# Decode attention with a parallel GLU on one Trainium2 core: head 0's K loaded in halves, two heads ahead of DVE's loop, eight rows of w_o on DVE, other pieces of w_down and w_o

## The chip, the cores and the metric

The kernel runs on one core of a Trainium2 chip. The core has five engines that run at the same time and tell each other of their progress by semaphores: PE (TensorE, matrix products), DVE (VectorE), ACT (ScalarE), POOL (GpSimd) and SP (SyncE, which here only issues transfers). 16 DMA engines bring data from the main memory into the core's own memory (128 partitions). The metric is the device time of one execution in microseconds (us), lower is better.

## The reference

One token is decoded. A cached attention and a gated feed-forward part both start from the same normalised input, and their outputs are added to it. All numbers are 32-bit floats.

```python
# x: (1,1,576); k_cache, v_cache: (1,32,16384,128); wq: (576,4096); wo: (4096,576)
# w_gate, w_up: (576,4608); w_down: (4608,576)
xn = layernorm(x)
q = (xn @ wq) as (1, 32 heads, 1, 128)
scores = einsum("bhqd,bhkd->bhqk", q, k_cache) * 128 ** -0.5
o = einsum("bhqk,bhkd->bhqd", softmax(scores), v_cache)
attention = o.reshape(1, 1, 4096) @ wo
h = gelu(xn @ w_gate) * (xn @ w_up)
return x + attention + h @ w_down
```

K and V of one head are 8.39 MB each, so 32 heads make 537 MB of the 588 MB that the kernel reads.

## The kernel before

The program writes out one list of instructions per engine (class `Plan`): `op` adds an instruction with the events it has to wait for, `dma` a transfer, `call` a hand-written loop. Every engine works through its list strictly in order. All large transfers are issued by SP, in the order of its list, to one queue.

Three large regions of memory, A, B and C, are used again and again. The input weights (wq, w_gate, w_up) lie in them first. Then K of even heads goes to region B (tile `kb`, which is `kt[0]`), K of odd heads to region A (`ka`, `kt[1]`), and V of every head to region C (`vt`). At the end the regions take w_down and w_o: `wd0` in B, `wd1` and `wo0` in A, `wo1` in B behind `wd0`, whose memory it uses again.

Start. PE computes q, the gate and the up part while the weights arrive (L210 to 253). The first K may be loaded when the gate part no longer needs region B (`done[0]`), the second K and the first V when the up part is through (`done[1]`). ACT writes the first head's q, spread over all partitions, to `qb0` (L277).

Heads. For each of 32 heads DVE (L302 to 315) waits for the head's K (semaphore `k0` or `k1`) and its q (`qb`), multiplies K by q in place (L308), sums over the 128 numbers of a key (L310, tile `sc`), and takes a maximum (L313, L315). `take` waits for a semaphore and takes its count back. With L312 (`s_kf`) DVE tells SP that the K tile is free. ACT makes the exponentials (L327), PE multiplies them with V (L292, "the PV product", tile `po`), ACT copies `po` out (L329) and PE folds it to one column per head (L297). With its first folding matmul PE tells SP (`s_vf`) that V's tile is free. So SP's order is V0, K2, V1, K3 and so on: K of head h + 2 waits for DVE's sums of head h, V of head h for the PV product of the head before.

Tail. The last transfers on SP's list are, in this order: V30, `wd0` (24 rows of w_down, when DVE has read K30), V31, `wd1` (12 rows, when DVE has read K31), three pieces of w_o of 6, 5 and 5 rows in region A, and eight pieces of 6, 4 and six times 1 row in region B, which wait until DVE has used `wd0`. A row here is 576 numbers on each of 128 partitions. DVE adds up the rows of w_down, each times a column of `hT`, in `wacc` (`down`, L355): first the rows of `wd0`, then, behind the normalisation of the attention output (L377 to L383, tile `oT`), the rows of `wd1`. PE takes the rows of w_o, two matmuls each (`out_rows`, L387): the first 26 into four groups of `acc`, the last six into `fin`. In PE's list the sum over the partitions of `wacc` goes to `fin` behind row 22 (`SUMS`), the sum of `acc` (copied to `part` by DVE, L403) behind row 27. DVE and ACT copy `fin` to `osb` (L406, L407), and SP stores it.

Of the kernel before, what the change touches and what calls it, by code (L numbers as in the profile page):

```python
# [9 lines left out]
ALU = mybir.AluOpType  # L10
AX = mybir.AxisListType
PE = mybir.EngineType.PE

P = 128
H, SK, DH = 32, 16384, 128
D, DF = 576, 4608
N = SK // P
# [8 lines left out]
WT = HD // P  # L26
CUT = ((0, 11), (11, 22), (22, 32))
S0 = 32512
SLOT = 4 * N * DH
WD1 = 24  # L30
WO1 = 16
WO_CUTS = (6, 5, 5, 6, 4, 1, 1, 1, 1, 1, 1)
LAST = 6
SUMS = 22


class Plan:
# [13 lines left out]
    def op(self, e, fn, *deps, sig=None, by=1):  # L51
        if e in ("dve", "act", "pool"):
            deps += (self.last.get(e),)
        sig = sig or self.own[e]
        self.count[sig.name] = self.count.get(sig.name, 0) + by
        self.q[e].append((deps, fn, sig, by))
        if sig is self.own[e]:
            self.last[e] = sig, self.count[sig.name]
        return sig, self.count[sig.name]

    def dma(self, e, out, in_, *deps, sem=None):
        sem = sem or self.sem(f"d{len(self.count)}")
        return self.op(e, lambda g: g.dma_start(out, in_), *deps, sig=sem, by=16)
# [27 lines left out]
def take(g, sem, n=1):  # L91
    g.wait_ge(sem, n).then_inc(sem, -n)  # L92
# [8 lines left out]
def plan(nc, pl, x, k_cache, v_cache, wq, wo, wg, wu, wd, out):  # L101
    op, dma = pl.op, pl.dma
    kv = k_cache.rearrange("b h (p n) d -> (b h) p (n d)", p=P)
# [23 lines left out]
    ident, ones = small("ident", [P, P]), small("ones", [P, P])  # L127
# [7 lines left out]
    qb = [small(f"qb{i}", [P, DH]) for i in range(2)]  # L135
    sc = [small(f"sc{i}", [P, N]) for i in range(2)]
    pm, nm, nb, pe = small("pm", [P, 1]), small("nm", [1, 1]), small("nb", [P, 1]), small("pe", [P, N])
    ls, o4 = small("ls", [P, H + 1]), small("o4", [P, 512])
    oall, oT = small("oall", [P, H + 1]), small("oT", [P, WT])
# [5 lines left out]
    wacc, part = small("wacc", [P, 2, HALF], over), small("part", [P, 2, HALF], over + 4 * D)  # L145
# [7 lines left out]
    kt = [big("kb", N * DH, B), big("ka", N * DH, A)]  # L153
    vt = big("vt", N * DH, C)
    wd0, wd1 = big("wd0", WD1 * D, B), big("wd1", (FT - WD1) * D, A)
    wo0, wo1 = big("wo0", WO1 * D, A + 4 * (FT - WD1) * D), big("wo1", (WT - WO1) * D, B)

# [5 lines left out]
    po, pqb, pt, pb, pc, acc, fin = banks(("po", 1), ("pqb", 1), ("pt", 1), ("pb", 1), ("pc", 1), ("acc", 2), ("fin", 1))  # L163
    px = pu[:, 0, :]

    s_hs, s_pm, s_nm, s_p, s_o4, s_v = (pl.sem(n) for n in ("hs", "pm", "nm", "p", "o4", "v"))
    s_pq, s_pt, s_pb, s_pv, s_pc = (pl.sem(n) for n in ("pq", "pt", "pb", "pv", "pc"))
    s_qb, s_ol, s_kf, s_vf, s_d, s_a = (pl.sem(n) for n in ("qb", "ol", "kf", "vf", "d", "a"))
    s_k = [pl.sem(f"k{i}") for i in range(2)]


# [21 lines left out]
    for i in range(2):  # L193
        k = op("dve", lambda g, i=i: g.bn_stats(st[:, i, :], xrow[:, i * HALF : (i + 1) * HALF]), d_x)
    k = op("dve", lambda g: g.bn_aggr(mv, st), k)
    k = op("act", lambda g: g.activation(std, mv[:, 1:2], AF.Sqrt, bias=eps[:1], scale=1.0), k, c_eps)
    k = op("dve", lambda g: g.reciprocal(rstd, std), k)
# [3 lines left out]
    for j in range(DJ):  # L201
        k = op("pe", lambda g, j=j: g.matmul(px[:, j : j + 1], xm[:, j, :], ones[:1, :1], start=True, stop=True), k_xn, c_ones)
    k = op("pe", lambda g: g.matmul(px[:, DJ : DJ + 1], xd.rearrange("o d s -> o (d s)"), ones[:1, :1], start=True, stop=True), k_xd)
    k = op("dve", lambda g: g.tensor_copy(xp, px[:, : DJ + 1]), k)
    k_xnb = op("dve", lambda g: g.tensor_copy(xnb, xp[:, :DJ].unsqueeze(2).to_broadcast([P, DJ, 32])), k)
    k = op("dve", lambda g: g.tensor_scalar(xt, par, xp[:, DJ:], None, op0=ALU.mult), k, c_par)
# [20 lines left out]
    rows = [(wqm[:, j * HD : (j + 1) * HD], d_q[0]) for j in range(DJ)]  # L227
# [18 lines left out]
    done = []  # L246
    for i, (dst, pieces, t) in enumerate(((pg, gp, (gt, d_g[2])), (pu, up, (ut, d_ut)))):
        view = []
        for b, (lo, hi) in enumerate(CUT):
            k = wide(dst, b, (FT * lo, FT * hi), pieces, t, FQ)  # L250
# [9 lines left out]
    k = op("dve", lambda g: g.tensor_mul(t1, g_, g_), k_f)  # L260
    k = op("dve", lambda g: g.tensor_scalar(t1, t1, 0.044715, 1.0, op0=ALU.mult, op1=ALU.add), k)
    k = op("dve", lambda g: g.tensor_mul(t1, t1, g_), k)
    k = op("act", lambda g: g.activation(th, t1, AF.Tanh, scale=0.7978845608028654), k)
    k = op("dve", lambda g: g.scalar_tensor_tensor(t2, th, 1.0, g_, op0=ALU.add, op1=ALU.mult), k)
    k_h = op("dve", lambda g: g.scalar_tensor_tensor(hT, t2, 0.5, u_, op0=ALU.mult, op1=ALU.mult), k)
# [9 lines left out]
    k = op("act", lambda g: pick(g, 0), c_h)  # L275
# [4 lines left out]
    def on_pe(g):  # L280
        with g.Fori(0, H):
# [17 lines left out]
                    m.then_inc(s_vf, 1)  # L299
            m.then_inc(s_pc, 1)  # L300

    def on_dve(g):  # L302
        with g.Fori(0, H // 2):  # L303
            for i in range(2):
                kd = kt[i].rearrange("p (n d) -> p n d", d=DH)
                take(g, s_k[i], 16)
                take(g, s_qb)
                g.tensor_mul(kd, kd, qb[i].unsqueeze(1).to_broadcast([P, N, DH])).then_inc(s_d, 1)  # L308
                take(g, s_d)
                g.tensor_reduce(sc[i], kd, axis=AX.X, op=ALU.add).then_inc(s_d, 1)  # L310
                take(g, s_d)
                g.sem_inc(s_kf, 1)  # L312
                g.tensor_reduce(pm, sc[i], axis=AX.X, op=ALU.max).then_inc(s_pm, 1)  # L313
                take(g, s_pt)
                g.tensor_reduce(nm, pt[:1, 0, :P], axis=AX.X, op=ALU.max, negate=True).then_inc(s_nm, 1)  # L315

    def on_act(g):
        with g.Fori(0, H, 2) as h2:
# [18 lines left out]
    def load_k(h, *deps):  # L337
        dma("sp", kt[h % 2], kv[h], *deps, sem=s_k[h % 2])
# [1 line left out]
    def load_v(h):  # L340
        dma("sp", vt, vv[h], (s_vf, h) if h else done[1], sem=s_v)

    load_k(0, done[0])
    load_k(1, done[1])
    for h in range(H - 2):
        load_v(h)
# [5 lines left out]
    k_o = s_ol, H  # L352


    def down(lo, hi, w, dep, k):  # L355
        for t in range(lo, hi):
            r, c = w[:, (t - lo) * D : (t - lo + 1) * D], hT[:, t : t + 1]
            o = wacc.rearrange("p a f -> p (a f)")
            if t == 0:
                k = op("dve", lambda g, r=r, c=c: g.tensor_scalar(o, r, c, None, op0=ALU.mult), dep, k_h)  # L360
            else:
                k = op("dve", lambda g, r=r, c=c: g.scalar_tensor_tensor(o, r, c, o, op0=ALU.mult, op1=ALU.add), dep, k)  # L362
        return k

    k_w0 = down(0, WD1, wd0, d_wd0, None)
    d_wo, lo = [], 0
    for n in WO_CUTS:
        w, base, dep = (wo0, 0, (s_kf, H)) if lo < WO1 else (wo1, WO1, k_w0)
        c = w[:, (lo - base) * D : (lo - base + n) * D]
        d = dma("sp", c, wov[:, lo * D : (lo + n) * D], dep)  # L370
# [5 lines left out]
    k = op("pe", lambda g: g.matmul(pqb[:, 0, :H], ones, ls[:, :H], start=True, stop=True))  # L376
    k = op("dve", lambda g: g.reciprocal(rl, pqb[:, 0, :H]), k)  # L377
    k = op("dve", lambda g: g.tensor_mul(oexp, oall[:, :H].unsqueeze(2).to_broadcast([P, H, 4]),
                                         rl.unsqueeze(2).to_broadcast([P, H, 4])), k, k_o)
    k = op("pe", lambda g: g.matmul(pt[:, 0, :P], oexp.rearrange("p h a -> p (h a)"), ident, start=True, stop=True), k)  # L380
    k = op("dve", lambda g: g.tensor_mul(ot, pt[:, 0, :P].rearrange("p (a t) -> p a t", a=4),
                                         m4.unsqueeze(2).to_broadcast([P, 4, 32])), k, c_m4)
    k_oT = op("dve", lambda g: g.tensor_reduce(oT, ot.rearrange("p a t -> p t a"), axis=AX.X, op=ALU.add), k)  # L383
    k_w1 = down(WD1, FT, wd1, d_wd1, k_w0)


    def out_rows(g_of, lhs, w, deps, start, stop, to=None):  # L387
        for a in range(2):
            o = acc[32 * g_of : 32 * g_of + 1, a, :HALF] if to is None else to[32 * a : 32 * a + 1, 0, :HALF]
            k = op("pe", lambda g, o=o, a=a: g.matmul(o, lhs, w[:, a * HALF : (a + 1) * HALF], start=start, stop=stop), *deps)  # L390
        return k

    out_rows(0, ones[:1, :1], xrow, (k_o,), True, False, fin)
    for t in range(WT):
        w, d = d_wo[t]
        if t < WT - LAST:
            k = out_rows(t % 4, oT[:, t : t + 1], w, (d, k_oT), t < 4, t >= WT - LAST - 4)
        else:
            k = out_rows(0, oT[:, t : t + 1], w, (d,), False, t == WT - 1, fin)
        if t == SUMS:  # L400
            out_rows(0, ones[:, 0:1], wacc.rearrange("p a f -> p (a f)"), (k_w1,), False, False, fin)
        if t == WT - LAST - 1:
            k_part = op("dve", lambda g: g.tensor_copy(part, acc[:, :, :HALF]), k, k_w1)  # L403
        if t == WT - LAST + 1:
            out_rows(0, m32[:, 0:1], part.rearrange("p a f -> p (a f)"), (k_part,), False, False, fin)
    k0 = op("dve", lambda g: g.tensor_copy(osb[:, 0, :], fin[:1, 0, :HALF]), k)  # L406
    k1 = op("act", lambda g: g.activation(osb[:, 1, :], fin[32:33, 0, :HALF], AF.Copy), k)  # L407
    d = dma("sp", of, osb.rearrange("o a f -> o (a f)"), k0, k1)
# [29 lines left out]
```

## Time and profile before

| what | value |
|---|---|
| median of 3 runs | 1366.36 us (1366.23 to 1368.02) |
| the profiled execution: its time | 1367.37 us |
| its span (first to last instruction in the profile) | 1365.6 us |
| DVE busy | 1170.1 us (86%) |
| PE busy | 425.5 us (31%) |
| read from main memory | 587.60 MB |
| K or V of one head | 8.39 MB |

Times in the trace are microseconds from the start of the span. In a row of the timeline stand the start, the busy time, the engine, the line of the program, the operation, the tile written and the tiles read, the shape, the number of instructions merged ("x23"), and in brackets how long the engine had been idle before and what ended it. A row of an issue answer gives the tile, the number of transfers and the time from the issue to the landing. SPq is SP's issuing of a transfer. "PEclk" or granted clock is the share of full speed at which PE was allowed to run.

### The profile page before, as it was taken

The numbers are of one execution on the slowest core, as the hardware profiler recorded it, in microseconds if no ns is written. First come the engines' busy times: TensorE is split into PE (matmuls) and PEld (weight loads), VectorE is DVE, ScalarE is ACT, GpSimd is POOL, SyncE is SP. The second block draws the span as 40 slices with busy tenths as digits, with TensorE's granted clock in tenths as the row PEclk, the third lists the DMA queues.
The fourth block names the chain that finished last, engine by engine and source line by source line (L and its number), as shares of the span: only waits on it lengthen the run. The fifth ranks groups of instructions, "written<-read, shape, count | busy, mean of one in ns | idle before, by whom it ended". The sixth has DMA issues, their size and how long they took to land. (4 is left out here: it accounts for less than half of the span.)

```text
span 1365.6 us, 7293 instructions
## 1 busy us (share of the span) xinstructions
PE 425.5 (31%) x2940; PEld 133.2 (10%) x2940; DVE 1170.1 (86%) x205; ACT 65.3 (5%) x232; POOL 0.7 (0%) x6
## 2 busy tenths in 40 slices
PE   3431233333222333333222333322213333332137
PEld 1110010111000111101000111100001111010002
DVE  1149999999998988898888888998888888998893
ACT  0000000000000000000000000000000000000000
POOL 0000000000000000000000000000000000000000
PEclk9765565665566566566556655665566566566558
DMA  9999999999999999999999999999999999999997
GB/s 399 434 436 428 435 440 436 432 432 432 434 432 430 443 436 432 432 436 432 430 442 438 432 432 436 432 430 440 440 432 430 434 434 432 430 447 432 426 430 330
DMA packets 12250, 587.69 MB, mean 430 GB/s; under 512 B 1362, under 2 KB 1362, under 8 KB 2132
## 3 DMA queue, kind: packets, MB, share of 16 engines
q1 hardware_dynamic: 12242, 587.60, 99.5%
q8 instruction: 4, 0.07, 0.0%
q14 instruction: 2, 0.02, 0.0%
q10 hardware_dynamic: 2, 0.00, 0.0%
HBM read 587.60 MB, written 0.00 MB: 430 GB/s over the span
## 5 line engine op out<-in xcount | busy, mean ns | idle before, releaser
L292 PE MATMUL po<-vt,pe 128*4 128x512 f32 x2048 | 293.6, 737 | 590.5 <-PEq L92 590.5
L308 DVE TENSOR_TENSOR kb<-kb,qb 128x16384 f32<-128x16384 f32 x16 | 275.6, 17226 | 33.6 <-DVEq L92 33.6
L308 DVE TENSOR_TENSOR ka<-ka,qb 128x16384 f32<-128x16384 f32 x16 | 275.6, 17226 | 32.5 <-DVEq L92 31.8
L310 DVE TENSOR_REDUCE sc<-ka 128x128 f32<-128x16384 f32 x16 | 275.5, 17220 | 2.3
L310 DVE TENSOR_REDUCE sc<-kb 128x128 f32<-128x16384 f32 x16 | 275.5, 17220 | 2.3
L292 PEld LDWEIGHTS po<-vt,pe 128*4 128x4 f32 x2048 | 56.6, 99 | 800.4 <-issue 800.4
L285 PE MATMUL pt<-ident,pm 128*1 128x128 f32 x32 | 11.9, 372 | 243.2 <-PEq L92 243.2
L329 ACT ACTIVATE o<-po 128x512 f32<-128x512 f32 x32 | 19.1, 597 | 857.9 <-ACTq L92 857.9
L297 PE MATMUL pc<-m,o 128*128 128x1 f32 x256 | 32.7, 249 | 28.9 <-PEq L92 28.9
L297 PEld LDWEIGHTS pc<-m,o 128*128 128x128 f32 x256 | 31.0, 191 | 57.7 <-issue 57.7
L362 DVE SCALAR_TENSOR_TENSOR wacc<-wd,hT,wacc 128x576 f32<-128x576 f32 x35 | 28.7, 819 | 1.3
L315 DVE TENSOR_REDUCE nm<-pt 1x1 f32<-1x128 f32 x32 | 8.9, 279 | 21.5 <-DVEq L92 21.5
L285 PEld LDWEIGHTS pt<-ident,pm 128*1 128x1 f32 x32 | 2.5, 79 | 248.5 <-issue 248.5
L287 PE MATMUL pb<-nm,ones 1*128 1x1 f32 x64 | 17.7, 343 | 18.5 <-PEq L92 18.5
L237 DVE TENSOR_TENSOR tmp<-pqs,m 128x1024 f32<-128x1024 f32 x1 | 1.2, 1224 | 25.2 <-PE pqs L224 25.2
L237 DVE TENSOR_TENSOR tmp<-pg,m 128x396 f32<-128x396 f32 (+1 forms) x3 | 1.7, 558 | 21.8 <-PE pg L224 21.8
L237 DVE TENSOR_TENSOR tmp<-pu,m 128x396 f32<-128x396 f32 (+1 forms) x3 | 1.7, 558 | 20.4 <-PE pu L224 20.4
L287 PEld LDWEIGHTS pb<-nm,ones 1*128 1x128 f32 x64 | 15.9, 306 | 27.9 <-issue 27.9
L325 ACT ACTIVATE nb<-pb 128x1 f32<-128x1 f32 x32 | 5.5, 171 | 274.3 <-ACTq L92 274.3
L224 PE MATMUL pg<-gm,xnb 128*32 128x396 f32 (+1 forms) x96 | 12.1, 651 | 11.8 <-DMA gm<-in_B_w_gate_dram 11.8
L313 DVE TENSOR_REDUCE pm<-sc 128x1 f32<-128x128 f32 x32 | 9.2, 286 | 7.6 <-DVEq L92 7.6
L283 PE MATMUL pqb<-qsel,hsel 128*128 128x128 f32 x64 | 15.3, 321 | 0.7 <-PEq L92 0.7
(83 smaller groups left out, 145.4 us busy)
## 6 DMA issues: line engine op xcount, KB each, us to landing
gm<-in_B_w_gate_dram SPq DMA_DIRECT2D x2, 4608.0 KB, 40.7
wd<-in_B_w_down_dram SPq DMA_DIRECT2D x1, 6912.0 KB, 39.2
ua<-in_B_w_up_dram SPq DMA_DIRECT2D x1, 4608.0 KB, 58.3
ub<-in_B_w_up_dram SPq DMA_DIRECT2D x1, 4608.0 KB, 39.2
wd<-in_B_w_down_dram SPq DMA_DIRECT2D x1, 3456.0 KB, 28.0
wo<-in_A_wo_dram SPq DMA_DIRECT2D x2, 1728.0 KB, 26.6
wo<-in_A_wo_dram SPq DMA_DIRECT2D x2, 1440.0 KB, 35.9
wo<-in_A_wo_dram SPq DMA_DIRECT2D x6, 288.0 KB, 24.4
```

Of the source, the lines that this page charges most:

```text
L224: k = op("pe", lambda g, o=o, a=args, j=j: g.matmul(o, *a, start=j == 0, stop=j == DJ), dep, k_x)
L283: g.matmul(pqb[:, 0, :DH], hsel, qsel, start=True, stop=True).then_inc(s_pq, 1)
L285: g.transpose(pt[:1, 0, :P], pm, ident).then_inc(s_pt, 1)
L287: g.matmul(pb[:, 0, :1], ones[:1, :], nm, start=True, stop=True).then_inc(s_pb, 1)
L292: m = g.matmul(po[q : q + 4, 0, :], pe[:, k : k + 4], vt[:, k * DH : (k + 4) * DH], start=k < 16, stop=k >= N - 16)
L297: m = g.matmul(pc[:, 0, :1], o4[:, j * DH : (j + 1) * DH], m32[:, j : j + 1], start=j == 0, stop=j == 3)
L308: g.tensor_mul(kd, kd, qb[i].unsqueeze(1).to_broadcast([P, N, DH])).then_inc(s_d, 1)
L310: g.tensor_reduce(sc[i], kd, axis=AX.X, op=ALU.add).then_inc(s_d, 1)
L313: g.tensor_reduce(pm, sc[i], axis=AX.X, op=ALU.max).then_inc(s_pm, 1)
L315: g.tensor_reduce(nm, pt[:1, 0, :P], axis=AX.X, op=ALU.max, negate=True).then_inc(s_nm, 1)
L329: g.activation(o4, po[:, 0, :], AF.Copy).then_inc(s_o4, 1)
L362: k = op("dve", lambda g, r=r, c=c: g.scalar_tensor_tensor(o, r, c, o, op0=ALU.mult, op1=ALU.add), dep, k)
```

## The change

Head 0's K is loaded by two transfers, the first 64 and the last 64 keys of every partition; the first has a semaphore of its own (`s_kh`). DVE multiplies the first half when it is there, then the second, and goes on as before. To write this, head 0 and head 1 stand in front of DVE's loop, which now runs 15 times over two heads instead of 16. `wd0` has 28 rows and `wd1` 8; w_o has 20 rows in region A and 12 in B, in pieces of 8, 8, 4 (A), 3, 2 and seven times 1 (B). The second piece of w_o, rows 8 to 15, is no longer used by PE: DVE multiplies each row by its column of `oT` and adds it to `wacc`, behind the rows of `wd1`. PE's list of rows is shorter by these eight, and the sum of `wacc` stands behind row 23.

```diff
-WD1 = 24
-WO1 = 16
-WO_CUTS = (6, 5, 5, 6, 4, 1, 1, 1, 1, 1, 1)
+WD1 = 28
+WO1 = 20
+WO_CUTS = (8, 8, 4, 3, 2, 1, 1, 1, 1, 1, 1, 1)
+ON_DVE = range(8, 16)
 LAST = 6
-SUMS = 22
+SUMS = 23
...
+    def products(g, i, n=(0, N)):
+        kd = kt[i].rearrange("p (n d) -> p n d", d=DH)[:, n[0] : n[1], :]
+        g.tensor_mul(kd, kd, qb[i].unsqueeze(1).to_broadcast([P, n[1] - n[0], DH])).then_inc(s_d, 1)
+        take(g, s_d)
+
+    def sums(g, i):
+        g.tensor_reduce(sc[i], kt[i].rearrange("p (n d) -> p n d", d=DH), axis=AX.X, op=ALU.add).then_inc(s_d, 1)
+        take(g, s_d)
+        g.sem_inc(s_kf, 1)
+        g.tensor_reduce(pm, sc[i], axis=AX.X, op=ALU.max).then_inc(s_pm, 1)
+        take(g, s_pt)
+        g.tensor_reduce(nm, pt[:1, 0, :P], axis=AX.X, op=ALU.max, negate=True).then_inc(s_nm, 1)
+
+    def scores(g, i):
+        take(g, s_k[i], 16)
+        take(g, s_qb)
+        products(g, i)
+        sums(g, i)
+
     def on_dve(g):
-        with g.Fori(0, H // 2):
+        take(g, s_kh, 16)
+        take(g, s_qb)
+        products(g, 0, (0, N // 2))
+        take(g, s_k[0], 16)
+        products(g, 0, (N // 2, N))
+        sums(g, 0)
+        scores(g, 1)
+        with g.Fori(0, H // 2 - 1):
             for i in range(2):
...
+                scores(g, i)
...
-    load_k(0, done[0])
+    dma("sp", kt[0][:, : N // 2 * DH], kv[0][:, : N // 2 * DH], done[0], sem=s_kh)
+    dma("sp", kt[0][:, N // 2 * DH :], kv[0][:, N // 2 * DH :], sem=s_k[0])
...
     k_w1 = down(WD1, FT, wd1, d_wd1, k_w0)
+    for t in ON_DVE:
+        k_w1 = op("dve", lambda g, r=d_wo[t][0], c=oT[:, t : t + 1]: g.scalar_tensor_tensor(
+            o_sum, r, c, o_sum, op0=ALU.mult, op1=ALU.add), d_wo[t][1], k_w1)
...
+    rows = [t for t in range(WT - LAST) if t not in ON_DVE]
     for t in range(WT):
         w, d = d_wo[t]
-        if t < WT - LAST:
-            k = out_rows(t % 4, oT[:, t : t + 1], w, (d, k_oT), t < 4, t >= WT - LAST - 4)
-        else:
+        if t in rows:
+            i = rows.index(t)
+            k = out_rows(i % 4, oT[:, t : t + 1], w, (d, k_oT), i < 4, i >= len(rows) - 4)
+        elif t not in ON_DVE:
             k = out_rows(0, oT[:, t : t + 1], w, (d,), False, t == WT - 1, fin)
         if t == SUMS:
-            out_rows(0, ones[:, 0:1], wacc.rearrange("p a f -> p (a f)"), (k_w1,), False, False, fin)
+            out_rows(0, ones[:, 0:1], o_sum, (k_w1,), False, False, fin)
```

More of the change, by code (lines that the diff above doesn't have):

```diff
@@ L168, in plan @@
     s_qb, s_ol, s_kf, s_vf, s_d, s_a = (pl.sem(n) for n in ("qb", "ol", "kf", "vf", "d", "a"))
+    s_kh = pl.sem("kh")
     s_k = [pl.sem(f"k{i}") for i in range(2)]
@@ L300, in on_pe @@
             m.then_inc(s_pc, 1)
-    def on_dve(g):
-        with g.Fori(0, H // 2):
-            for i in range(2):
[L305 to L315, printed above, removed]
+    def products(g, i, n=(0, N)):
[14 more added lines that the diff above has]
+        sums(g, i)
+    def on_dve(g):
+        take(g, s_kh, 16)
[6 more added lines that the diff above has]
+        with g.Fori(0, H // 2 - 1):
+            for i in range(2):
+                scores(g, i)
     def on_act(g):
@@ L352, in plan @@
     k_o = s_ol, H
+    o_sum = wacc.rearrange("p a f -> p (a f)")
     def down(lo, hi, w, dep, k):
@@ L357, in down @@
             r, c = w[:, (t - lo) * D : (t - lo + 1) * D], hT[:, t : t + 1]
-            o = wacc.rearrange("p a f -> p (a f)")
             if t == 0:
-                k = op("dve", lambda g, r=r, c=c: g.tensor_scalar(o, r, c, None, op0=ALU.mult), dep, k_h)
+                k = op("dve", lambda g, r=r, c=c: g.tensor_scalar(o_sum, r, c, None, op0=ALU.mult), dep, k_h)
             else:
-                k = op("dve", lambda g, r=r, c=c: g.scalar_tensor_tensor(o, r, c, o, op0=ALU.mult, op1=ALU.add), dep, k)
+                k = op("dve", lambda g, r=r, c=c: g.scalar_tensor_tensor(o_sum, r, c, o_sum, op0=ALU.mult, op1=ALU.add), dep, k)
         return k
```

## The prediction

> **What bounds the kernel now.** I read the page first.
>
> ```profile
> span 1365.6 us, 7293 instructions
> DMA packets 12250, 587.69 MB, mean 430 GB/s; under 512 B 1362, under 2 KB 1362, under 8 KB 2132
> q1 hardware_dynamic: 12242, 587.60, 99.5%
> DMA wo<-in_A_wo_dram 2%; DVE wacc L362 1%; PE acc L390 0%; PE fin L390 0%; DVE wacc L360 0%; DVE osb L406 0%; DVE nm L315 0%; DVEq L303 0%; DVEq L79 0%
> ```
>
> One queue keeps the 16 DMA engines at work for 99.5% of the span, and the bytes are not changed. So only two things can be won or lost: moments in which transfers stop, and what runs after the last transfer. The chain names the w_o transfers and the work on their rows. Next comes the timeline of the start, with the issue-to-landing answers for K0 (issued 59.94), V0 (84.62), K2 (130.03) and V1 (144.93), in this order.
>
> ```profile
> 59.94 0.33 SPq L63 DMA_DIRECT2D kb<-in_A_k_cache_dram  x1
> 84.62 0.43 SPq L63 DMA_DIRECT2D vt<-in_A_v_cache_dram  x1
> 92.53 0.28 ACT L277 ACTIVATE qb<-pqb 128x128 f32<-128x128 f32 x1 [0.88 <-PE pqb L276]
> 95.26 17.23 DVE L308 TENSOR_TENSOR kb<-kb,qb 128x16384 f32<-128x16384 f32 x1 [3.96 <-DVEq L92]
> 112.63 17.22 DVE L310 TENSOR_REDUCE sc<-kb 128x128 f32<-128x16384 f32 x1
> 130.03 0.33 SPq L63 DMA_DIRECT2D kb<-in_A_k_cache_dram  x1
> 144.93 0.33 SPq L63 DMA_DIRECT2D vt<-in_A_v_cache_dram  x1
> ```
>
> ```profile
> kb<-in_A_k_cache_dram SPq DMA_DIRECT2D x1, 35.1
> vt<-in_A_v_cache_dram SPq DMA_DIRECT2D x1, 49.0
> kb<-in_A_k_cache_dram SPq DMA_DIRECT2D x1, 24.5
> vt<-in_A_v_cache_dram SPq DMA_DIRECT2D x1, 28.9
> ```
>
> K0 lands at 59.94 + 35.1 = 95.04, V0 at 133.62, K2 at 154.53, V1 at 173.83. From K2 to V1 one load of 8.39 MB takes 19.3 us; from V0 to K2 it takes 20.9. K2 was issued only 3.6 us before V0 had landed, and the windows of 3 us show the dip:
>
> ```profile
> 130.00:133.00 3.00, 0.93 (x3) 0.57 (x3) 1.85 (x3) 0.66 (x3) 0.00 (x0) 0.50 0.83 328
> ```
>
> In the 3 us from 130 the DMA engines' share (last column but one) is 0.83, and they move 328 GB/s instead of the mean 430. That late K2 is the only stop of the stream I see: V1 was issued 9.6 us before K2 landed. Then the tail, and behind it how long the first w_down piece (issued 1271.59), V31 (1305.63) and the last w_o row took to land:
>
> ```profile
> 1271.59 0.33 SPq L63 DMA_DIRECT2D wd<-in_B_w_down_dram  x1
> 1305.63 0.33 SPq L63 DMA_DIRECT2D vt<-in_A_v_cache_dram  x1
> 1312.15 19.61 DVE L362 SCALAR_TENSOR_TENSOR wacc<-wd,hT,wacc 128x576 f32<-128x576 f32 x23
> 1330.28 8.96 PE L292 MATMUL po<-vt,pe 128*4 128x512 f32 x64 [17.98 <-PEq L92]
> 1339.40 0.60 ACT L329 ACTIVATE o<-po 128x512 f32<-128x512 f32 x1 [26.12 <-ACTq L92]
> 1343.05 0.37 DVE L383 TENSOR_REDUCE oT<-ot 128x32 f32<-128x128 f32 x1
> 1343.52 10.22 DVE L362 SCALAR_TENSOR_TENSOR wacc<-wd,hT,wacc 128x576 f32<-128x576 f32 x12
> 1353.41 3.42 PE L390 MATMUL acc<-wo,oT 128*1 128x288 f32 x25 [1.98 <-DMA wo<-in_A_wo_dram]
> 1356.21 0.65 PE L390 MATMUL fin<-wacc,ones 128*1 128x288 f32 x2
> 1360.15 2.11 PE L390 MATMUL fin<-wo,oT 128*1 128x288 f32 x16
> 1362.33 0.45 DVE L406 COPY osb<-fin 1x288 f32<-1x288 f32 x1 [2.72 <-PE fin L390]
> ```
>
> ```profile
> wd<-in_B_w_down_dram SPq DMA_DIRECT2D x1, 6912.0 KB, 39.2
> vt<-in_A_v_cache_dram SPq DMA_DIRECT2D x1, 24.5
> ```
>
> ```profile
> 1341.26 2.96 SPq L63 DMA_DIRECT2D wo<-in_A_wo_dram  x1
> wo<-in_A_wo_dram SPq DMA_DIRECT2D x1, 288.0 KB, 19.2
> ```
>
> The first 24 rows of w_down land at 1271.59 + 39.2 = 1310.8, V31 at 1305.63 + 24.5 = 1330.1, and PE starts head 31's PV product 0.15 later. From there to oT: 13.3 us (1343.42). The last w_o row lands at 1341.26 + 19.2 = 1360.46, and the copy to osb starts at 1362.33. The sum of wacc was ready (1353.74) before PE came to it (1356.21), so today DVE holds up nobody; the end is the stream of rows plus a PE lag of over 1 us.
>
> **The change part by part, in the time scale of the old trace.**
>
> K0 in halves. The first half lands near 75.7 + 9.7 = 85.4 (K0's 19.3 us end at 95.04), before qb0 is there at 92.81. DVE then starts 0.2 after qb0, as it now starts 0.2 after K0: 93.0 instead of 95.26. The second half has landed when the first product ends (about 101.7). One more product costs one more gap of 0.14 (95.26 + 17.23 to 112.63) and a little start-up. So K2 is issued about 2.05 us earlier, near 128.0. The added transfer issue costs SP 0.33, hidden in SP's wait until 84. The unrolled two heads cost nothing I can find; DVE's instructions in them are the same.
>
> What the earlier K2 is worth: at most all of the 20.9 - 19.3 = 1.6 us. At least, if the slowest DMA engine is another one that lost less, the dip: (430 - 328)/430 x 3 = 0.7. The lead needed is about what the engines ran dry for, under 2 us, so I expect the stop to vanish. I take **-1.1**, the middle. V1 still waits for V0's landing and PE, so nothing else moves, and after it every landing comes 1.1 earlier.
>
> w_down 28 + 8 instead of 24 + 12. Four rows (4 x 128 x 576 x 4 B = 1.18 MB) move in the queue from behind V31 to in front of it. At 430 GB/s that is 2.74 us: they land at 1313.5, some 1.9 us after DVE is free for them (one row ahead of 1312.15); 28 rows at 0.853 (19.61/23) then end near 1337.4. SP releases the last 12 rows of w_o then; their turn is over 10 us later, so that delay is covered. But V31 lands **+2.74** later, and PV, oT and everything of DVE behind oT with it. Before, this would not have mattered; now it does, since DVE gets the longest work in the tail:
>
> DVE's eight w_o rows. After oT DVE has 8 rows of w_down and 8 of w_o, 16 instead of 12. All have landed (the second piece ends sixteen rows of 0.69, as below, before the last: near 1348). At 10.22/12 = 0.852 a row it is **13.6** instead of 10.2 us. In numbers: oT at 1343.42 - 1.1 + 2.74 = 1345.06; head 31's PV product varies:
>
> ```profile
> 133.75 9.89 PE L292 MATMUL po<-vt,pe 128*4 128x512 f32 x64 [1.72 <-PEq L92]
> 1256.01 8.55 PE L292 MATMUL po<-vt,pe 128*4 128x512 f32 x64 [20.98 <-PEq L92]
> ```
>
> With the middle of these, 9.2, instead of 8.96, oT is at 1345.3, DVE done at 1345.4 + 13.6 = 1359.0.
>
> Where PE meets it. PE's order puts the wacc sum behind row 23. Row 23 is eight rows before the end, so it lands near 1360.5 - 1.1 - 8 x 0.69 = 1353.9 (one row is 0.295 MB) and PE, eight rows lighter, is at the sum by 1355.5 to 1357. There it now waits for DVE until **1359.0**, and rows 24 to 31, the copy of part and its sum are queued behind that wait. This is the new bound: the rows have landed by 1359.4 and no longer matter. The pieces of one row thus buy nothing. SP's issue of the last one blocked for 2.96 us, and with nine pieces behind 1337 instead of eight it may block longer; the cover is that PE asks for row 31 only near 1364, 4 us behind its landing, and without it a late row would cost what it is late.
>
> What is left behind the wait: wacc, rows 24 and 25, rows 26 and 27, part, rows 28 to 31. Rows 28 to 31 took 2.11 us as 16 records, two side by side, so about 0.243 a step. The list is 2 + 4 + 4 + 2 + 8 = 20 steps = 4.85, plus 0.1 for the part copy and 0.2 to osb: **5.15 at full clock**. The clock is the last term:
>
> ```profile
> 1341.01:1344.42 3.41, 2.33 (x26) 1.00 1.01 430
> 1344.42:1347.83 3.41, 3.41 (x31) 0.50 1.01 432
> 1347.83:1351.25 3.42, 3.04 (x30) 1.00 0.99 424
> 1351.25:1354.66 3.41, 1.43 (x21) 1.00 0.98 402
> 1354.66:1358.07 3.41, 3.41 (x24) 0.50 0.96 378
> 1358.07:1361.49 3.42, 3.42 (x32) 1.00 0.13 52
> ```
>
> These windows (columns: length, PE busy, granted clock, DMA share, GB/s) follow the clock's steps. After a window with PE busy for 2.33 or 1.43 us the clock is 0.5, after one with 3.04 or more it is full. In the changed tail PE idles about 2 us or more before the sum, so the window behind it is half empty, and the sum begins at 0.5. It stays there till the end of the first window that is about three quarters full, 2.5 to 5.9 us, and half of that is lost: 1.2 to 2.9, I take **+1.9**. That the PV products spread by 1.3 us is the same thing.
>
> The Trainium skill, "TensorE: Matmul & The Clock Gate", section "What's actually happening", has the clock fall to half after at least one idle window of about 3.4 us. By it the wait, about 2 to 3.5 us, would mostly leave the clock full, and the sum would be without the 1.9. The trace here disagrees: the clock fell at 1354.66 though the longest idle stretch before was 1.98 us.
>
> The sum: osb starts at 1359.0 + 5.15 + 1.9 = 1366.05 instead of 1362.33, **+3.7 us**. The profiled execution took 1367.37 (1.8 around its span), and would be 1371.1; the median of the runs is 1366.36, 1.0 below, and would be 1370.1. The clock's phase differs from run to run and the three runs reach to 1368.02, so I put the forecast at **1370.4**.
>
> **The rivals.** (1) The forecast: PE stalls at the wacc sum and goes on at half clock: 1368.9 to 1371.9. Chance 0.57.
>
> (2) The same stall, full clock behind it, or a PV product at its short end: +3.7 - 1.9 = +1.8, that is 1368.2. For it: the stall is short. Against it: the two falls in the windows above. 0.25.
>
> (3) The stop at K2 stays, because its first packets and not its issue are slow: +3.7 + 1.1 = +4.8, that is 1371.5. Against it: the stream is full at every load issued with more lead. 0.13.
>
> (4) Faster: DVE is not late, and the tail ends with the last row. It decides from DVE being done by about 1355, which needs (1355 - 1345.4)/16 = 0.6 us a row, or V31 not delayed. Then the last row lands at 1359.4, PE ends 0.5 later and osb starts near 1360.2: -2.1, 1364.3; with the whole 1.6 at the front 1363.8, and 1363.6 would be 0.2% faster. Against it: 35 rows at 0.85, and landings in order of issue all through the tail. 0.05.
>
> **How the numbers follow.** About 0.2% (2.7 us) is what a measurement of this kernel can tell from no change, so slower begins at 1369.1. (3) and nearly nine tenths of (1) lie above: 0.64. Within: (2), the low end of (1) and half of (4): 0.33. Faster: 0.03. Unknown terms: front 0.7 to 1.6, PV -0.6 to +0.7, clock 1.2 to 2.9 (0 in rival 2), base 1366.2 to 1368. Range 1367.5 to 1372.3; without (2) it would be 1368.9 to 1372.
>
> **What will show it.** Right: DVE's first product near 93.0 and K2 issued near 128.0; V0 to K2 landing 19.4; the first w_down piece landing near 1312.4 and V31 near 1331.8 on the span's scale; 16 rows of DVE behind oT, ended near 1359; PE idle over 2 us before fin<-wacc with DVE as releaser, then clock 0.5; the chain of waits through DVE's w_o rows instead of w_o transfers. Wrong: PE waiting for a w_o transfer behind row 23, a row price of DVE under 0.8, a full clock behind the sum, or a K2 that still lands 20.9 after V0.

## The result, and the profile after

| kernel | median us | runs | profiled execution us | its span us |
|---|---|---|---|---|
| before | 1366.56 (1366.11 to 1368.02) | 10 | 1367.37 | 1365.6 |
| changed | 1369.93 (1369.44 to 1372.08) | 10 | 1369.94 | 1368.1 |

The ratio is 1.0027 (95% interval 1.0017 to 1.0037): the change makes the kernel 3.4 us slower by the medians, 2.5 us by the two spans. The forecast was 1370.4.

The page of the changed kernel:

```profile
span 1368.1 us, 7241 instructions
q1 hardware_dynamic: 12530, 587.60, 99.3%
DVE wacc L382 0%; DVE wacc L406 0%; PE fin L413 0%; PE acc L413 0%; PE pc L299 0%; PE pt L400 0%; DVE osb L431 0%; DVE oT L403 0%; DVE rl L397 0%; DVE ot L401 0%; DVE oexp L398 0%; PE pqb L396 0%; DVEq L80 0%
```

The same bytes move, but the chain that ended last no longer holds a transfer of w_o. It runs through the PV fold of head 31, oT, DVE's rows of w_down (L382) and of w_o (L406), and PE. The start, with the landing answers of V0 (issued 84.92) and K2 (128.43):

```profile
84.92 0.43 SPq L64 DMA_DIRECT2D vt<-in_A_v_cache_dram  x1
93.25 8.69 DVE L306 TENSOR_TENSOR kb<-kb,qb 128x8192 f32<-128x8192 f32 x1 [1.65 <-DVEq L93]
102.20 8.69 DVE L306 TENSOR_TENSOR kb<-kb,qb 128x8192 f32<-128x8192 f32 x1 [0.26 <-DVEq L93]
128.43 0.33 SPq L64 DMA_DIRECT2D kb<-in_A_k_cache_dram  x1
```

```profile
vt<-in_A_v_cache_dram SPq DMA_DIRECT2D x1, 48.8
kb<-in_A_k_cache_dram SPq DMA_DIRECT2D x1, 24.8
```

DVE starts on the first half at 93.25 instead of 95.26, though V0's issue and `qb0` come 0.3 us later in this execution. K2 is issued at 128.43 instead of 130.03, and lands at 153.23, 19.5 us behind V0 (133.72) where it was 20.9. From K2 to V1 one load took 19.3 before, so 0.2 us of the stop in the stream is left. The tail, and then the answers for V31 (issued 1303.40) and for the last row of w_o:

```profile
1303.40 0.33 SPq L64 DMA_DIRECT2D vt<-in_A_v_cache_dram  x1
...
1311.96 0.52 DVE L380 TENSOR_SCALAR wacc<-wd,hT 128x576 f32<-128x576 f32 x1 [2.05 <-DMA wd<-in_B_w_down_dram]
...
1331.39 8.67 PE L294 MATMUL po<-vt,pe 128*4 128x512 f32 x64 [20.78 <-PEq L93]
...
1343.86 0.37 DVE L403 TENSOR_REDUCE oT<-ot 128x32 f32<-128x128 f32 x1
1344.33 6.80 DVE L382 SCALAR_TENSOR_TENSOR wacc<-wd,hT,wacc 128x576 f32<-128x576 f32 x8
...
1351.24 6.80 DVE L406 SCALAR_TENSOR_TENSOR wacc<-wo,oT,wacc 128x576 f32<-128x576 f32 x8
...
1358.09 0.66 PE L413 MATMUL fin<-wacc,ones 128*1 128x288 f32 x4 [2.43 <-DVE wacc L406]
1358.57 2.10 PE L413 MATMUL acc<-wo,oT 128*1 128x288 f32 x8
1360.44 1.92 PE L413 MATMUL fin<-wo,oT 128*1 128x288 f32 x8
...
1362.68 2.11 PE L413 MATMUL fin<-wo,oT 128*1 128x288 f32 x16
...
1364.87 0.45 DVE L431 COPY osb<-fin 1x288 f32<-1x288 f32 x1 [3.33 <-PE fin L413]
```

```profile
vt<-in_A_v_cache_dram SPq DMA_DIRECT2D x1, 27.9
```

```profile
1345.44 2.27 SPq L64 DMA_DIRECT2D wo<-in_A_wo_dram  x1
```

```profile
wo<-in_A_wo_dram SPq DMA_DIRECT2D x1, 288.0 KB, 13.5
```

V31 lands at 1331.30; before it was 1330.13, although V31 is now issued 2.2 us earlier: four more rows of w_down lie ahead of it in the queue. DVE has 16 rows from 1344.33 to 1358.04. PE stands idle for 2.43 us in front of the sum of wacc, released by L406. The last row of w_o lands at 1358.94, 0.85 us after the sum's start, but it stands at the end of PE's list, whose last four rows begin at 1362.68. From the sum's start to osb it takes 6.8 us. The windows of the granted clock (length, PE busy, clock, DMA share, GB/s):

```profile
1348.36:1351.77 3.41, 1.18 (x16) 1.00 0.99 416
1351.77:1355.18 3.41, 2.66 (x15) 0.50 1.03 406
1355.18:1358.60 3.42, 0.99 (x8) 1.00 0.66 252
1358.60:1362.01 3.41, 3.41 (x18) 0.50 0.00 0
```

PE was busy for only 0.99 us of the window to 1358.60, and for the next 3.4 us it is granted half its clock: there lie rows 24 to 27, and only behind it the steps are short again (16 records in 2.11 us, where 8 took 2.10 and 1.92).

### The profile page after: what moved, and what is told of

It reads as the page before. It is cut to its first block, busy times and chain, and to the rows that moved or that the text cites. A ratio compares the mean times of both kernels' runs of the same rounds, so it can differ in the third digit from the quotient of the medians.

```text
span 1368.1 us, 7241 instructions
## 1 busy us (share of the span) xinstructions
PE 421.1 (31%) x2908; PEld 131.5 (10%) x2908; DVE 1176.7 (86%) x214; ACT 65.4 (5%) x232; POOL 0.7 (0%) x6
## 5 line engine op out<-in xcount | busy, mean ns | idle before, releaser
L306 DVE TENSOR_TENSOR kb<-kb,qb 128x16384 f32<-128x16384 f32 (+1 forms) x17 | 275.8, 16221 | 32.8 <-DVEq L93 32.8
L382 DVE SCALAR_TENSOR_TENSOR wacc<-wd,hT,wacc 128x576 f32<-128x576 f32 x35 | 28.7, 819 | 1.3
```

The lines of the kernel that those rows point to most:

```text
L306: g.tensor_mul(kd, kd, qb[i].unsqueeze(1).to_broadcast([P, n[1] - n[0], DH])).then_inc(s_d, 1)
L382: k = op("dve", lambda g, r=r, c=c: g.scalar_tensor_tensor(o_sum, r, c, o_sum, op0=ALU.mult, op1=ALU.add), dep, k)
```

## The experiments

The experiments were timed in three groups, each on a chip of its own, and the kernel before was timed with each group on the same chip: medians 1366.86 (front, tail, sums behind the last row, no row on DVE), 1366.31 (four rows, w_down as before, the first trial of the spare matmuls) and 1366.46 (the last two). Differences are taken to the one of the same group.

**The front alone.** The old constants and no row on DVE:

```diff
-WD1 = 28
-WO1 = 20
-WO_CUTS = (8, 8, 4, 3, 2, 1, 1, 1, 1, 1, 1, 1)
-ON_DVE = range(8, 16)
+WD1 = 24
+WO1 = 16
+WO_CUTS = (6, 5, 5, 6, 4, 1, 1, 1, 1, 1, 1)
+ON_DVE = range(0)
...
-SUMS = 23
+SUMS = 22
```

> The front of the change alone (head 0's K in halves, two heads ahead of DVE's loop) with the old tail. Theory (K2's late issue let the DMA engines run dry; the gain reaches the end): 1.1 to 1.6 us faster than the kernel before, K2 landing 19.4 to 19.6 us behind V0 instead of 20.9, every later landing 1.1 to 1.6 us earlier. Rival (the gap at K2 is hidden again later, or its first packets are slow whatever the lead): 0 to 0.3 us.

Measured: 1364.99 us, 1.9 below the kernel before and 0.3 past the end of what I expected; ratio 0.999 (0.9981 to 0.9999). In its trace V0 landed at 133.77, K2 was issued at 128.39 and V31 at 1303.32; the answers for these two:

```profile
kb<-in_A_k_cache_dram SPq DMA_DIRECT2D x1, 24.7
```

```profile
vt<-in_A_v_cache_dram SPq DMA_DIRECT2D x1, 25.2
```

K2 lands 19.3 us behind V0, so the whole stop of 1.6 us is gone, and V31 lands at 1328.52, 1.6 us before that of the kernel before (1330.13). The gain at K2 is carried through all heads; the rival of a hidden gain falls. The medians differ by 0.3 us more than the landings of V31; that rest is not explained.

**The tail alone.** Head 0 as it was:

```diff
-    s_kh = pl.sem("kh")
...
-        take(g, s_kh, 16)
-        take(g, s_qb)
-        products(g, 0, (0, N // 2))
-        take(g, s_k[0], 16)
-        products(g, 0, (N // 2, N))
-        sums(g, 0)
-        scores(g, 1)
-        with g.Fori(0, H // 2 - 1):
+        with g.Fori(0, H // 2):
...
-    dma("sp", kt[0][:, : N // 2 * DH], kv[0][:, : N // 2 * DH], done[0], sem=s_kh)
-    dma("sp", kt[0][:, N // 2 * DH :], kv[0][:, N // 2 * DH :], sem=s_k[0])
+    load_k(0, done[0])
```

> The tail of the change alone (w_down 28 + 8, w_o's new pieces, eight rows on DVE, the wacc sum behind row 23), with head 0 as before. Theory (tail costs the stall at the wacc sum plus half clock behind it, and the front took 1.1 to 1.6 of it back): 4.5 to 5.1 us slower than before, DVE's last w_o row near 1359.5, PE waiting for it over 2 us. Rival (the front gave nothing): 3.2 to 3.6 us slower.

Measured: 1372.56 us, 5.7 above; ratio 1.0042 (1.0028 to 1.0056). It is 0.6 above the upper end that I gave, and the two parts add up: +5.7 - 1.9 = +3.8, against 3.4 to 3.7 for the whole change. The sum of wacc and the copy to osb in its timeline, and the clock windows:

```profile
1360.80 1.13 PE L404 MATMUL fin<-wacc,ones 128*1 128x288 f32 x4 [4.48 <-DVE wacc L397]
...
1368.21 0.40 ACT L423 ACTIVATE osb<-fin 1x288 f32<-1x288 f32 x1 [23.47 <-PE fin L404]
```

```profile
1351.88:1355.29 3.41, 2.32 (x29) 1.00 1.02 412
1355.29:1358.70 3.41, 1.03 (x4) 1.00 0.97 377
1358.70:1362.11 3.41, 1.31 (x6) 0.50 0.11 43
1362.11:1365.53 3.42, 3.42 (x16) 0.50 0.00 0
```

PE waits 4.48 us for DVE, and here the clock stays at half for 4.7 us of what follows: 7.4 us from the sum to osb.

**The sums behind the last row.** Is it the wait in PE's list that costs, or do the transfers come too late? Only the place of the two sums is changed:

```diff
-            k = out_rows(0, oT[:, t : t + 1], w, (d,), False, t == WT - 1, fin)
-        if t == SUMS:
-            out_rows(0, ones[:, 0:1], o_sum, (k_w1,), False, False, fin)
+            k = out_rows(0, oT[:, t : t + 1], w, (d,), False, False, fin)
...
-        if t == WT - LAST + 1:
-            out_rows(0, m32[:, 0:1], part.rearrange("p a f -> p (a f)"), (k_part,), False, False, fin)
+    out_rows(0, ones[:, 0:1], o_sum, (k_w1,), False, False, fin)
+    k = out_rows(0, m32[:, 0:1], part.rearrange("p a f -> p (a f)"), (k_part,), False, True, fin)
```

> The changed kernel with the sums of wacc and part behind row 31 in PE's list, nothing else moved: DVE's sum comes as late as before (near 1358.0), but no row of w_o is queued behind it. Theory (the loss is PE's wait in front of rows 24 to 31): osb starts between 1360.7 (full clock) and 1362.2, 2.5 to 4 us faster than the changed kernel, so 0 to 1.6 us faster than the kernel before. Rival (the loss is in the transfers: V31 and the rows land too late, or DVE's rows slow them): still 3 us or more slower than before.

Measured: 1365.88 us, 1.0 below the kernel before; ratio 0.9994 (0.9985 to 1.0003), not clear of it, but 4.4 us better than the changed kernel against its own. DVE's timeline and PE's:

```profile
1352.86 6.80 DVE L406 SCALAR_TENSOR_TENSOR wacc<-wo,oT,wacc 128x576 f32<-128x576 f32 x8
```

```profile
1359.71 0.65 PE L413 MATMUL fin<-wacc,ones 128*1 128x288 f32 x4
...
1361.30 0.45 DVE L429 COPY osb<-fin 1x288 f32<-1x288 f32 x1 [0.78 <-PE fin L413]
```

DVE ends at 1359.66, even 1.6 us later than in the changed kernel, and osb starts 3.6 us earlier. So the loss is not that DVE is late or that V31 and the rows land late, but that eight rows and part stood behind the wait. This order has a price too: the two sums, 1.6 us from their start to osb, now stand behind the last row, and the version with no row on DVE, next, is 1.3 us faster.

**No row on DVE.**

```diff
-ON_DVE = range(8, 16)
+ON_DVE = range(0)
```

> The changed kernel with all 32 rows of w_o on PE; w_down 28 + 8 and the new pieces stay, V31 stays late. Theory: DVE is done with 8 rows near 1351, before PE comes to the sum, nobody waits for it; the end is the last row's landing (1358.9) plus PE's lag, osb at 1359.9 to 1361.3, so 1.0 to 2.4 us faster than the kernel before and 3.5 to 5 faster than the changed one. Rival (V31's later landing alone is the loss): 2 us or more slower than before.

Measured: 1364.62 us, 2.2 below; ratio 0.9985 (0.9976 to 0.9994). This version beats both kernels; by its own base it is 5.6 us better than the changed kernel, 0.6 past the end of what I expected. DVE's and PE's timeline:

```profile
1344.20 6.80 DVE L382 SCALAR_TENSOR_TENSOR wacc<-wd,hT,wacc 128x576 f32<-128x576 f32 x8
```

```profile
1353.76 0.40 PE L413 MATMUL acc<-wo,oT 128*1 128x288 f32 x1 [0.22 <-DMA wo<-in_A_wo_dram]
1353.77 0.41 PE L413 MATMUL fin<-wacc,ones 128*1 128x288 f32 x2
...
1359.47 0.45 DVE L431 COPY osb<-fin 1x288 f32<-1x288 f32 x1 [3.11 <-PE fin L413]
```

DVE is done at 1351.0, PE comes to the sum at 1353.77, side by side with row 23 (the row above it), and doesn't wait. The later V31 costs nothing by itself. Next to the front alone it is 0.4 us faster, so w_down's new cut and w_o's new pieces do no harm and may gain a little; the two medians are too close to call that.

**Four rows on DVE.**

```diff
-ON_DVE = range(8, 16)
+ON_DVE = range(8, 12)
```

> The changed kernel with four rows of w_o on DVE (rows 8 to 11) instead of eight. Theory (the loss begins only where DVE's end passes PE's arrival at the sum, near 1355): DVE has 12 rows behind oT, is done near 1354.6, PE waits less than 0.5 us, and the time is that of the kernel with no row on DVE, 1364.5 to 1365.6. Rival (each row on DVE costs its 0.85 us): 3.4 us faster than the changed kernel only, 1366.5 or more.

Measured: 1365.69 us, 0.6 below; ratio 0.9995 (0.9986 to 1.0004), 0.1 over the upper end that I gave. Row 23, the sum and osb:

```profile
1353.76 1.13 PE L413 MATMUL acc<-wo,oT 128*1 128x288 f32 x4 [0.22 <-DMA wo<-in_A_wo_dram]
1355.05 0.65 PE L413 MATMUL fin<-wacc,ones 128*1 128x288 f32 x4 [0.16 <-DVE wacc L406]
...
1360.27 0.45 DVE L431 COPY osb<-fin 1x288 f32<-1x288 f32 x1 [2.72 <-PE fin L413]
```

PE is idle for 0.16 us only, but that is counted from the end of row 23. With no row on DVE the sum began beside row 23, at 1353.77; here it begins 1.3 us later, and osb 0.8 us later (1360.27 against 1359.47). So four rows already lie past the point from which DVE decides, which I had put near 1355. Against the kernel before, no row on DVE gives -2.2, four rows -0.6 and eight +3.4: the first four cost 1.6 us, the next four 4.0. It is not a price per row. Of the 1.6, the traces show 0.8; the rest is not explained, and the runs with four rows spread widely (1364.56 to 1366.56, with no row 1364.51 to 1364.84).

**w_down cut as before, eight rows on DVE.**

```diff
-WD1 = 28
-WO1 = 20
+WD1 = 24
+WO1 = 16
```

> The changed kernel with w_down cut 24 + 12 as before (16 rows of w_o in region A; the same pieces of w_o, eight rows on DVE). V31 no longer lies behind four more rows of w_down, but DVE has 20 rows behind oT. Theory (both terms count: V31 2.7 us earlier, four rows 3.4 us more): DVE's sum 0.7 us later than in the changed kernel, time 1370.0 to 1371.5. Rival one (V31's place in the queue does not matter to DVE's end): 3.4 us slower, 1373 or more. Rival two (V31's place is most of the loss): 1368 or less.

Measured: 1372.08 us, 5.8 above; ratio 1.0043 (1.003 to 1.0057). It lies between theory and the first rival, so the time alone doesn't decide; the trace does (V31 issued 1302.76, its answer, oT and DVE's last rows):

```profile
vt<-in_A_v_cache_dram SPq DMA_DIRECT2D x1, 25.7
```

```profile
1342.16 0.37 DVE L403 TENSOR_REDUCE oT<-ot 128x32 f32<-128x128 f32 x1
1342.63 10.21 DVE L382 SCALAR_TENSOR_TENSOR wacc<-wd,hT,wacc 128x576 f32<-128x576 f32 x12
1352.95 6.80 DVE L406 SCALAR_TENSOR_TENSOR wacc<-wo,oT,wacc 128x576 f32<-128x576 f32 x8
```

V31 lands at 1328.46, 2.84 us earlier than in the changed kernel (the four rows: 2.74 by the prediction), and DVE needs 17.1 us for 20 rows. But from V31 to oT it took 14.1 us here and 12.9 there, so oT is only 1.7 earlier, and DVE ends at 1359.75, 1.7 later. Both terms are there; the other 1.1 us between V31 and oT goes with PE's clock, whose granted mean over that stretch was 0.74 here and 0.87 there.

**Spare matmuls in front of the sum.** Ten matmuls whose result nobody reads keep PE at work during its wait:

```diff
+WARM = 10
...
         if t == SUMS:
+            for _ in range(WARM):
+                op("pe", lambda g: g.matmul(pqb[:, 0, :DH], ident, ones, start=True, stop=True))
             out_rows(0, ones[:, 0:1], o_sum, (k_w1,), False, False, fin)
```

> The changed kernel with ten spare matmuls (128x128, into a bank that nothing reads any more) in PE's list between row 23 and the wacc sum: PE has work while it would wait for DVE, which is done as late as before. They add work that the result doesn't use. Theory (half of the granted clock behind the wait is a term of the loss): the windows before the sum are busy, the sum and rows 24 to 31 run at full clock, osb starts 5.2 us behind the sum's start instead of 6.8, and the kernel is 1.2 to 2.2 us faster than the changed one, 1367.7 to 1368.8. Rival (the clock is full there anyway, as after an idle stretch shorter than a window): 1369.4 to 1370.4, no gain.

Measured: 1369.19 us (1368.39 to 1369.71), 2.9 above the kernel before where the changed kernel is 3.4 above; ratio 1.0019 (1.001 to 1.0028). That is less than I expected, and not decisive, as runs of both fall into two clusters 1 to 2 us apart. So the two were timed once more, side by side.

> The changed kernel once more, beside the one with the spare matmuls on the same chip, because the two were not timed together before. Both theories: 1369.4 to 1371.5, with the phase of PE's clock windows deciding within this.

> The changed kernel with ten spare matmuls in front of the wacc sum once more. Theory (half clock behind the wait costs 1.2 to 2.2 us, less in runs whose windows happen to turn full early): mean 0.9 to 1.9 us below that of the changed kernel beside it. Rival (no clock term): within 0.3 us of it.

Measured: the changed kernel 1370.17 (7 runs, mean 1370.60), with the spare matmuls 1368.58 (11 runs, mean 1368.80). The gain is 1.6 us by the medians, 1.8 by the means, as the theory had it; the slowest run with the spare matmuls (1369.60) lies 0.02 above the fastest without (1369.58). The sum and osb, first of the changed kernel, then with the spare matmuls:

```profile
1359.42 1.13 PE L413 MATMUL fin<-wacc,ones 128*1 128x288 f32 x4 [4.33 <-DVE wacc L406]
...
1366.80 0.45 DVE L431 COPY osb<-fin 1x288 f32<-1x288 f32 x1 [3.46 <-PE fin L413]
```

```profile
1354.92 2.50 PE L428 MATMUL pqb<-ones,ident 128*128 128x128 f32 x20
1359.15 0.65 PE L414 MATMUL fin<-wacc,ones 128*1 128x288 f32 x4 [1.74 <-DVE wacc L407]
...
1364.37 0.44 DVE L434 COPY osb<-fin 1x288 f32<-1x288 f32 x1 [2.72 <-PE fin L414]
```

DVE releases the sum at nearly the same moment; from there it is 7.4 us without and 5.2 us with work for PE ahead of it. PE works more and the kernel is faster: the half clock is a term of the loss.

## Why the prediction was right

- **The front**, forecast -1.1 between 0.7 and 1.6: K2's lead came as worked out (issue 128.43 against 128.0, K2 19.5 us behind V0 against 19.4), and the gain was 1.6 in the traces (V31 of the front alone, 1328.52 against 1330.13); from the tail alone to the changed kernel it was 1.3 (V31 1332.59 and 1331.30). The term was sized too small: I discounted it for a slowest DMA engine that might not gain, but in the front alone the landing gained all of the gap.
- **w_down 28 + 8**, forecast +2.74 on V31's landing: V31 landed 1.17 later than before, which with the 1.6 of the front is 2.8; the cut back to 24 moved it 2.84. DVE's wait for the first piece was 2.05 us against 1.9, and hidden as said.
- **DVE's 16 rows**, forecast 13.6 us, end 1359.0: they took 13.7 (1344.33 to 1358.04). They ended 1.0 earlier than forecast because the front gave 0.5 more than the 1.1 and the PV product took 8.67 instead of the middle of 9.2.
- **PE at the sum**, forecast to arrive at 1355.5 to 1357 and wait: it was idle from 1355.66 on and waited 2.43 us, with DVE's L406 as releaser.
- **Behind the wait**, forecast 5.15 at full clock + 1.9: 6.8 here, 7.4 in two other executions, and 5.2 with the spare matmuls (all three in the lines above). That the sum would begin at half clock was not so in the profiled execution: the clock fell 0.5 us behind its start.
- **The rule of the Trainium skill** ("TensorE: Matmul & The Clock Gate", section "What's actually happening") that at least one idle window of 3.4 us brings half clock would have kept it full behind a wait of 2.43 us. Here it fell at 1358.60 after that wait, and filling the wait gave 1.6 us: with the measurement, a partly busy window is enough.

Altogether 1364.87 - 1362.33 = 2.5 us in the profiled executions, and 3.4 in the medians, where 3.7 was forecast. The profiled execution before lay 0.8 above its median, the one after on its median; that is the difference between the two figures. That the median came within 0.5 us of the forecast is in part luck: in the profiled execution osb starts 1.2 us earlier than the 1366.05 of the sum, 1.0 of it because DVE ended early, and single runs of the changed kernel lie from 1369.44 to 1372.08.

## What to carry to other kernels

PE takes its list in order, and paid for a late operand with everything that stood behind it: before work is moved to a second engine, compare that engine's end with the moment at which the first engine asks for the sum, and put the sum as late as the data of the rest allow. Eight rows taken off PE put 6.8 us onto DVE, which had 2.8 us to spare behind oT (1351.0 against 1353.77 with no row); the same change without them is 2.2 us faster than the kernel before. The gap in the stream at the first head, 1.6 us, was still worth its full length when V31 landed.

## What the runs showed that I had not expected

In the tail a share of busy time does not settle the next clock. In the kernel with the tail alone a window with PE busy for 2.32 us was followed by full clock, in the kernel before one with 2.33 us by half. Under the heads, where the PV product is most of PE's work, it does: cut into the clock's windows of 3.41 us, the eleven traces hold 3641 between 160 and 1290 us, and behind each of them the clock was half where PE had been busy for less than 2.50 us, and full where it had been for more than 2.52. Which of the matmuls in a window of the tail count, and how much, was not tried.
